# Whole-array state reads, batch 1 by half products, and a new order of all steps in an attention and PReLU-MLP kernel

## The chip, the cores and the metric

The kernel runs on one core of one Trainium2 chip. The metric is device time in microseconds (us) of one execution, the median over runs. The core has five engines with an instruction stream of their own each: TensorE (PE; its weight loads are listed as PEld), VectorE (DVE), ScalarE (ACT), GpSimd (POOL) and SyncE (SP, which here only issues DMAs). Each engine works through its stream in order and waits on semaphores for the others.

## The reference

Input x is (8 batches, 8 heads, 512 tokens, 64), state is (8, 8, 32, 64). Each batch and head computes attention both ways between its 512 tokens and its 32 states. The 544 rows of each batch, 512 wide, then go through an MLP with a leaky activation.

```python
scores = scale * np.matmul(x, state.transpose(0, 1, 3, 2))
a = softmax(scores)
xread = np.matmul(a, state)
scores2 = scale * np.matmul(state, x.transpose(0, 1, 3, 2))
a2 = softmax(scores2)
sread = np.matmul(a2, x)
x = concat([xread, sread], axis=2) as (4352, 512)
h = x @ w_in
g = np.maximum(h, 0.0) + alpha * np.minimum(h, 0.0)
return g @ w_out
```

(softmax over the last axis; d_ff is 2048; inputs and output are float32.)

## The kernel before

All matmuls take float16 and accumulate in float32. The work is cut into named steps, and one long string, `ORDER` (lines 17 to 96), lists them. Every token calls one function, which puts its instructions at the end of the streams of the engines it uses; there is no other scheduler. So the order of tokens is the order of work on each engine, DMA queues included. Numbers behind a step are batch, tile, part and PSUM bank (0 to 5; a further double bank is called "two"); a letter names the engine (a ACT, v DVE, p POOL).

**Loading.** Batch 0's x comes by two float32 loads from SP and is cast on chip (`cx`). The other batches (`lx`), the states (`lst`) and the MLP's weights in four parts each (`wi`, `wo`) come by POOL's queue, which casts on the way. In an x tile `xg` the token at j, p, r (two halves, 128 partitions, two neighbours) lies in partition p. `alpha` comes as a (128, 16) tile.

**Attention, tokens to states.** x is transposed, for batches 0 and 1 on PE (`xt`, copied by `xo`), for the others by a DMA (`xd`). `sc` are the scores, tiled onto parts of the PE array. `sb` (DVE block transpose), `smax`, `ssh` (shift, on POOL), `sexp` (ACT), `ssum`, `snorm` and `wb` (transpose back) make the weights `aT`. Batch 0 has another way, with scores per token (`tsc`) and PE transposes (`at`, `ao`). The token read is never formed: `m` multiplies the states of a batch by w_in (`mo` casts the result), and a first step takes aT times that.

**The MLP.** `F.b.jc` computes 128 columns of h for 512 tokens with two 512-column matmuls. `N` (ACT, relu of -h) and `G` (DVE) make g of it. `f`, `n`, `g` are the same by halves for batch 0's first columns. Batches 0 and 1 use `S.b.q.jc2`: two 512-column matmuls that accumulate an output tile, which `O` copies and stores. Batches 2 to 8 (8 stands for the state rows of all batches) use seven products of half matrices in place of eight (`P`, four 256-column matmuls each), with sums of w_out halves (`W`, on POOL, once) and of g halves (`U.b.i.c`, on POOL). `K` keeps a partial result in SBUF and `Q` adds it and stores a quarter.

**State reads.** `tm`, `nb`, `te`, `tsum`, `tn` make the softmax over tokens, `tt` transposes it by a DMA (SP) into `e2T`, and `rd` multiplies x by it. Each of its 32 matmuls has 64 columns of weights and 32 moving columns; the two heads of a pair lie side by side in the array (`tile_position=(0, D * i)`). `rdo` copies the result to `XS` on ACT, where the first steps of "batch 8" read it.

`Z.k.n` are n matmuls on a made-up pattern whose result nobody reads.

Of the kernel before, what the change touches and what calls it, by code (L numbers as in the profile page):

```python
# [21 lines left out]
xt.1.1.1.0 xt.1.0.0.3 wo.3 te.0.1 tsum.0 xo.1.0.0.v oma mo.0.0.a.0 m.1.0 f.0.1.0.4 sexp.0.1 ssum.0.1 xo.1.1.1.v  # L22
mo.1.0.a n.0.1.0 xt.1.0.1.1 xo.1.0.1.v f.0.0.0.2 n.0.0.0 xt.1.1.0.5 xo.1.1.0.v g.0.1.0.1 g.0.1.0.0 m.2.0.3.0 m.1.1
mo.1.1.a snorm.p.0.1 at.1.1 mo.2.0.a.0 ao.1.v g.0.0.0.1 m.0.1.5.4 mo.0.1.a.0 sc.1 tm.1 f.0.1.1.1 f.0.0.1.3 mo.0.1.a.1
F.0.4.5 F.0.5.4 mo.2.0.a.1 n.0.0.1 nb.1.a n.0.1.1 sb.1 te.1.0 g.0.0.0.0 g.0.1.1.0 te.1.1 S.0.2.1.0 g.0.1.1.1 F.0.6.2
N.0.6 g.0.0.1.1 g.0.0.1.0 tsum.1 G.0.6 N.0.5 G.0.5 S.0.2.0 S.0.1.1.1 m.0.2 mo.0.2.a F.0.7.3 N.0.7 smax.1 S.0.1.0 N.0.4
G.0.4 F.0.10.2 N.0.10 m.0.3 G.0.7 mo.0.3.a F.0.11.4 G.0.10 N.0.11 G.0.11 F.0.9.5 m.1.3 N.0.9 G.0.9 F.0.13.3 N.0.13
tn.0.1.p F.0.8.2 S.0.1.5 F.0.12.4 S.0.3.1.5 S.0.2.5 N.0.8 G.0.13 N.0.12 ssh.p.1 wo.1 sexp.1 F.0.15.3 S.0.3.5 G.0.8
S.0.2.4 mo.1.3.a G.0.12 ssum.1.2 F.0.14.4 S.0.2.6 S.0.1.6 m.1.2 S.0.3.6 S.0.3.4 snorm.v.1 lx.2 xd.2 wb.1 tn.1.1.a
S.0.1.4 W.1.1.p S.0.2.2 S.0.1.3 F.1.3.2 tn.0.0.a tt.0 mo.1.2.a N.0.14 S.0.2.3 G.0.14 N.0.15 G.0.15 F.1.10.4 F.1.2.3  # L30
tn.1.0.p N.1.3 G.1.3 N.1.2 G.1.2 S.0.2.7 O.0.2.a tt.1 S.0.3.0 N.1.10 F.1.4.2 N.1.4 G.1.10 G.1.4 S.0.1.7 F.1.9.0
F.1.11.3 N.1.9 G.1.9 F.1.1.4 N.1.1 G.1.1 S.0.1.2 N.1.11 W.3.0.p G.1.11 S.0.3.2 F.1.6.2 N.1.6 S.0.3.7 O.0.1.a sc.2 tm.2
m.2.2.0.4 rd.0.3 mo.2.2.a.1 sb.2 mo.2.2.a.0 rdo.0.a F.1.15.1 N.1.15 W.1.0.p G.1.15 nb.2.a S.0.0.5.4 F.1.8.0 N.1.8
# [66 lines left out]
def kernel(  # L100
# [118 lines left out]
    def fill(k, n):  # L219
        t = single(k, f"fill_{len(zs)}", [128, 256], F32)  # L220
# [565 lines left out]
```

## Time and profile before

| | us |
|---|---|
| runs (3) | 213.7, 214.05, 214.37 |
| median | 214.05 |
| profiled execution, first to last instruction (span) | 212.2 |

A time of its own is not listed for the profiled execution; the median stands 1.85 us above its span. Busy in that span: PE 203.6, DVE 174.8, POOL 165.0, ACT 150.3 us. The granted TensorE clock is 1.000.

In the views quoted below, a window row gives a stretch and its length, then the busy time of PE, PEld, DVE, ACT and POOL with their numbers of instructions, the clock, the busy share of the DMA engines and GB/s. A row of the chain gives start, duration, engine, tile and line. A timeline row gives start, duration, engine, line, operation, output and inputs, shape, count, and in brackets the idle time before and what ended it. A group row gives engine, operation, tiles, shape and count, then busy us and mean ns, then idle time before it and who ended that. In a row of waits stand total us, number and the longest.

### The profile page before, as it was taken

The page shows a single profiled execution, that of the slowest core. Times are in us where ns is not written, and L with a number is a line of the kernel's source. Part 1 is how long each engine was busy: PE and PEld are TensorE (multiplying, and loading weights), DVE is VectorE, ACT ScalarE, POOL GpSimd, SP SyncE. Part 2 cuts the span into 40 slices and gives each one's busy share as a digit, 9 for nine tenths or more (in the row PEclk, how much of TensorE's full clock was granted, in tenths as well). Part 3 has the DMA queues.
Part 4 walks back from the last instruction along what each step waited for, and adds up shares of the span by engine and source line. Part 5 has one row for each costly group of instructions (what it writes and reads, how often), then busy time and mean ns, then how long its engine had stood idle before and what let it go on. Part 6 is the DMA issues. An engine that isn't in the chain of part 4 may idle for free.

```text
span 212.2 us, 4985 instructions
## 1 busy us (share of the span) xinstructions
PE 203.6 (96%) x1974; PEld 132.5 (62%) x1974; DVE 174.8 (82%) x260; ACT 150.3 (71%) x292; POOL 165.0 (78%) x106
## 2 busy tenths in 40 slices
PE   7989899989999999999999999999999999999993
PEld 5655234444444545766668776767777678888882
DVE  0789999889999999999999999899997997423221
ACT  2489998789999869987998578878773866312110
POOL 8343074946749898969989999799979995999960
PEclk9999999999999999999999999999999999999999
DMA  6999979879599299634115581141305200121142
GB/s 172 208 183 205 207 114 163 127 186 114 172 111 258 29 150 149 151 78 123 53 49 57 95 249 48 21 131 21 82 8 145 102 0 0 53 99 49 43 158 99
DMA packets 52438, 23.68 MB, mean 112 GB/s; under 512 B 38464, under 2 KB 51392, under 8 KB 52416
## 3 DMA queue, kind: packets, MB, share of 16 engines
q0 software_dynamic: 18816, 8.09, 30.2%
q1 hardware_dynamic: 33328, 15.22, 28.5%
q8 instruction: 15, 0.25, 0.4%
q10 hardware_dynamic: 272, 0.07, 0.1%
q14 instruction: 7, 0.06, 0.1%
HBM read 17.31 MB, written 8.91 MB: 124 GB/s over the span
## 4 chain that ended last, share of the span: by engine, by line
PE 86%; DVE 6%; ACT 4%; DMA 2%; issue 1%; POOL 0%; POOLq 0%; ACTq 0%; DVEq 0%; SPq 0%
PE h L543 23%; PE px L701 21%; PE o L613 11%; PE pv L701 10%; PE py L701 5%; PE m_ps L494 4%; PE fill L223 4%; PE h L552 3%; PE sr_ps L467 2%; DMA e2T<-e 2%; DVE mx L368 1%; DVE g L599 1%; ACT m L520 1%; PE sc L303 1%; PE xT_ps L288 1%; ACT neg L596 1%
## 5 line engine op out<-in xcount | busy, mean ns | idle before, releaser
L599 DVE SCALAR_TENSOR_TENSOR g<-neg,oma_sb,h 128x512 f16<-128x512 f32 (+1 forms) x140 | 92.5, 710 | 9.5 <-ACT neg L596 8.3
L596 ACT ACTIVATE neg<-h 128x512 f32<-128x512 f32 (+1 forms) x140 | 75.3, 583 | 22.3 <-PE h L543 13.3
L543 PE MATMUL h<-aT,m 128*128 128x512 f16 x248 | 67.7, 379 | 1.3 <-DVE g L599 0.6
L701 PEld LDWEIGHTS <-gsum 128*128 128x128 f16 x416 | 40.3, 98 | 11.5 <-issue 1.3
L543 PEld LDWEIGHTS <-m 128*128 128x128 f16 x248 | 23.4, 98 | 20.1 <-issue 3.3
L701 PEld LDWEIGHTS <-g 128*128 128x128 f16 x312 | 30.3, 98 | 8.7 <-issue 0.8
L680 POOL TENSOR_TENSOR gsum<-g,g 128x1024 f16<-128x1024 f16 (+1 forms) x14 | 27.8, 1986 | 7.1 <-DVE g L599 4.8
L613 PE MATMUL o<-w_out_sb,g 128*128 128x512 f16 x128 | 33.1, 379 | 0.0
L680 POOL TENSOR_TENSOR gsum<-g,gsum 128x1024 f16<-128x1024 f16 (+1 forms) x14 | 27.8, 1991 | 1.9 <-PE px L701 1.6
L680 POOL TENSOR_TENSOR gsum<-g 128x1024 f16<-128x1024 f16 (+1 forms) x14 | 27.7, 1993 | 1.9 <-issue 1.9
L680 POOL TENSOR_TENSOR gsum<-gsum,g 128x1024 f16<-128x1024 f16 (+1 forms) x14 | 27.8, 1989 | 1.0
L701 PE MATMUL px<-ws,gsum 128*128 128x256 f16 x208 | 28.0, 273 | 0.0
L373 POOL TENSOR_TENSOR ts<-ts,mx 128x1024 f32<-128x1024 f32 x7 | 13.4, 1911 | 11.9 <-DVE mx L368 11.9
L613 PEld LDWEIGHTS <-g 128*128 128x128 f16 x128 | 12.2, 98 | 15.6 <-issue 1.2
L520 ACT CAST m<-m_ps 128x512 f16<-128x512 f32 x35 | 19.3, 598 | 3.7 <-PE m_ps L494 3.6
L717 ACT COPY kept<-px 128x512 f32<-128x512 f32 (+1 forms) x16 | 9.0, 566 | 14.1 <-PE px L701 11.0
L734 DVE TENSOR_TENSOR oq<-pv,kept 128x512 f32<-128x512 f32 (+1 forms) x14 | 9.1, 650 | 10.1 <-PE pv L701 7.2
L701 PE MATMUL pv<-ws,gsum 128*128 128x256 f16 x104 | 14.8, 273 | 0.0
L701 PE MATMUL px<-w_out_sb,g 128*128 128x256 f16 x104 | 14.6, 273 | 0.0
L701 PE MATMUL px<-w_out_sb,gsum 128*128 128x256 f16 x104 | 14.6, 273 | 0.0
L701 PE MATMUL py<-w_out_sb,g 128*128 128x256 f16 x104 | 14.5, 273 | 0.0
L701 PE MATMUL pv<-ws,g 128*128 128x256 f16 x104 | 14.3, 273 | 0.0
(74 smaller groups left out, 258.4 us busy)
## 6 DMA issues: line engine op xcount, KB each, us to landing
out_dram<-oq SPq DMA_DIRECT2D x24, 256.0 KB, 2.1
xg<-in_x_dram POOLq DMA_DIRECT2D x7, 512.0 KB, 6.1
w_in_sb<-in_moe_w_in_dram POOLq DMA_DIRECT2D x4, 512.0 KB, 14.3
w_out_sb<-in_moe_w_out_dram POOLq DMA_DIRECT2D x4, 512.0 KB, 14.0
out_dram<-osb SPq DMA_DIRECT2D x8, 256.0 KB, 3.1
x<-in_x_dram SPq DMA_DIRECT2D x2, 512.0 KB, 4.9
out_dram<-oq SPq DMA_DIRECT2D x4, 128.0 KB, 2.1
st<-in_state_dram POOLq DMA_DIRECT2D x1, 224.0 KB, 8.1
```

Source lines behind the costliest of these rows:

```text
L223: nc.tensor.matmul(t, pattern[:, :128], pattern, start=True, stop=True)
L373: engine(e).tensor_tensor(blocks(cols(live["ts", b], j, S)), blocks(scored(b, j)), over_blocks(cols(live["mx", b], j, S // N)), ALU.subtract,)
L494: nc.tensor.matmul(t[N * k : N * (k + 1), :], st_head(b, h)[64 * r : 64 * r + 64, :], w_in_sb[64 * r : 64 * r + 64, c, 512 * f : 512 * (f ...
L520: copier(e)(m_tile(b, f)[:, g, :], t[g])
L543: nc.tensor.matmul(h.rearrange("p (r j s) -> p r j s", r=2, j=2), ms[b, f][:, g, 128 * j : 128 * (j + 1)], weights(b, g), start=(g == 0), ...
L596: nc.scalar.activation(neg, h, RELU, bias=0.0, scale=-1.0)
L599: nc.vector.scalar_tensor_tensor(g_tile(b, jc), negs.pop((b, jc)), oma_sb[:, jc : jc + 1], hs.pop((b, jc)), ALU.mult, ALU.add,)
L613: nc.tensor.matmul(outs[b, q], g_tile(b, jc)[:, 128 * q : 128 * (q + 1)], w_out_sb[:, jc, :], start=not begun and jc == 2 * jc2, stop=left ...
L680: engine(e).tensor_tensor(t, x(), y(), op)
L701: nc.tensor.matmul(pbanks[b, name][:, i, :], of(b, c)[:, j, 128 * i : 128 * (i + 1)], moving[:, 4 * c + j, :], start=not begun and j == 0, ...
L717: copier(e)(t, pbanks[b, "x"])
L734: nc.vector.tensor_tensor(osb, pbanks[b, name], kept[b, add], ALU.add)
```

## The change

- **State reads.** Each matmul loads 128 neighbouring columns of x, its own 64 and the 64 beside them, and writes all 128 partitions. The head of a pair that wants the upper half starts 64 columns earlier. The result has a column block for each head of a pair, and only the half of the partitions that belongs to it is copied, so there are two copies per batch (16 in all, 14 on ACT and 2 on DVE).
- **Batch 1** uses the seven half products: 32 `S` and 4 `O` go, 28 `P`, 8 `U`, 3 `K` and 4 `Q` come.
- **Sums.** 15 of the 64 `U` are on DVE: one of batch 5, three of batch 6, four of batch 7 and seven of batch 8. The 8 `W` stay on POOL.
- **x in 1 KB runs.** The token at p, j, r is now row 4p + 2j + r, so a partition's four tokens lie together in memory; the output rows follow.
- **First x in four loads**: each half by two loads of four heads each, one on SP's queue and one on ACT's, the states between them on ACT's.
- **alpha** comes by four loads of 128-byte rows and is transposed on DVE.
- **Fills** have 512 columns; there are 6 at first and single ones later, where there were 16 of 256 and threes.
- **All places anew**: `ORDER` is another list of steps, with other banks and in part other engines.

The order before and after, up to batch 0's first read and the first w_out loads:

```diff
-wi.0 cx.0.1.a Z.0.3 cx.0.0.v Z.0.3 cx.1.0.v stc.a Z.0.3 stt.0 xt.0.0.1.1 Z.2.3 xt.0.0.0.2 cx.1.1.a xt.0.1.1.3 sbd.1.v
-lst lx.1 wi.1 wo.0 wi.2 xt.0.1.0.4 sbd.0.a xo.0.0.1.v tsc.0.1.5 xo.0.0.0.v tsc.0.0 wi.3 sto.v sc.0.0 xo.0.1.1.a
-xo.0.1.0.v sc.0.1 smax.0.0 ssh.v.0.0 sexp.0.0 tsc.1.0.1 Z.2.3 tm.0 Z.2.3 m.0.0.2.0 Z.3.3 mo.0.0.a.1 ssum.0.0 Z.3.3
-str.0.3 Z.4.3 tsc.1.1 str.1.4 nb.0.a te.0.0 sro.0.a smax.0.1 sro.1.v ssh.v.0.1 snorm.p.0.0 at.0.5 wo.2 ao.0.v
...
+Z.1.1 cx.0.0.v cx.0.1.v xt.0.0.0.2 xo.0.0.0.a xt.0.0.1.3 Z.4.1 stc.a Z.5.1 stt.0 cx.1.1.a sbd.1.a cx.1.0.v xt.0.1.0.1
+xo.0.1.0.a lst sbd.0.v xt.0.1.1.4 xo.0.0.1.v xo.0.1.1.a tsc.0.0.2 sto.a oma tsc.0.1 str.0.5 sro.0.a smax.0.0 ssh.v.0.0
+sexp.0.0 sc.0.1 sc.0.0 tm.0 wi.0 Z.3.1 lx.1 wi.1 wo.0 wi.2 ssum.0.0 snorm.p.0.0 str.1.1 tsc.1.0.4 sro.1.a tsc.1.1
+Z.0.1 smax.0.1 m.0.0.2.3 mo.0.0.v.1 Z.5.1 m.2.0.0.1 ssh.v.0.1 nb.0.a te.0.0 wi.3 te.0.1 tsum.0 tn.0.0.p mo.2.0.a.1
+at.0.5 tn.0.1.p ao.0.v sexp.0.1 m.1.0 mo.1.0.a mo.0.0.v.0 xt.1.0.1.3 xt.1.1.0.4 xo.1.0.1.v mo.2.0.a.0 ssum.0.1
+snorm.p.0.1 xt.1.0.0.1 xo.1.0.0.v f.0.1.0.5 f.0.0.0.2 xt.1.1.1.3 xo.1.1.1.v Z.0.1 n.0.0.0 g.0.0.0.0 m.1.1 m.0.1.1.0
+n.0.1.0 xo.1.1.0.v g.0.1.0.0 tt.0 mo.1.1.a at.1.3 ao.1.a sc.1 wo.1 g.0.1.0.1 Z.4.1 mo.0.1.a.0 W.1.0.p f.0.0.1.5
+f.0.1.1.3 mo.0.1.a.1 F.0.5.4 F.0.6.1 g.0.0.0.1 tm.1 sb.1 nb.1.v n.0.0.1 rd.0.2 g.0.0.1.0 n.0.1.1 N.0.5 G.0.5 S.0.2.1.0
+N.0.6 S.0.2.0 te.1.0 g.0.1.1.1 G.0.6 te.1.1 F.0.7.4 N.0.7 m.0.2 mo.0.2.a g.0.0.1.1 S.0.3.0.1 F.0.4.5 rdo.0.1.a lx.2
+wo.2 rdo.0.0.a g.0.1.1.0 N.0.4 S.0.3.1 smax.1 F.0.10.3 N.0.10 F.0.11.2 N.0.11 G.0.7 ssh.p.1 m.0.3 mo.0.3.a G.0.4
+tsum.1 G.0.10 F.0.9.4 N.0.9 G.0.11 F.0.8.5 G.0.9 N.0.8 G.0.8 S.0.2.2 tn.1.0.p S.0.3.3 F.0.12.3 N.0.12 G.0.12 F.0.15.2
...
```

The code:

```diff
-            x[b].rearrange("k (j p r) d -> p k j (r d)", j=2, r=2),
+            x[b].rearrange("k (p j r) d -> p k j (r d)", j=2, r=2),
...
-    def load_x0():
-        xgs[0] = att.tile([128, H, 2, 2, D], F16, name="xg_0", tag="xg", bufs=3)
-        for j in range(2):
-            t = att.tile([128, H, 2, D], F32, name=f"x0_{j}", tag="ts", bufs=2)
-            nc.sync.dma_start(
-                t, x[0, :, 256 * j : 256 * (j + 1), :].rearrange("k (p r) d -> p k r d", r=2)
-            )
+    def load_x0(j):
+        if j == 0:
+            xgs[0] = att.tile([128, H, 2, 2, D], F16, name="xg_0", tag="xg", bufs=3)
+        t = att.tile([128, H, 2, D], F32, name=f"x0_{j}", tag="ts", bufs=2)
+        x0s.append(t)
+        rows = x[0].rearrange("k (p j r) d -> j p k r d", j=2, r=2)[j]
+        for g in range(2):
+            queue = nc.sync if g == 0 else nc.scalar
+            queue.dma_start(t[:, 4 * g : 4 * g + 4], rows[:, 4 * g : 4 * g + 4])
...
-    alpha_sb = consts.tile([128, n_jc], F32)
-    nc.sync.dma_start(alpha_sb, moe_alpha.rearrange("(jc p) -> p jc", p=128))
-    pattern = consts.tile([128, 256], F16)
+    alpha_rows = consts.tile([128, 32], F32)
+    nc.vector.memset(alpha_rows, 0.0)
+    alpha_quarters = moe_alpha.rearrange("(jc q c) -> q jc c", q=4, c=32)
+    for q in range(4):
+        nc.sync.dma_start(alpha_rows[32 * q : 32 * q + n_jc, :], alpha_quarters[q])
+    pattern = consts.tile([128, 512], F16)
...
-    fill(0, 16)
+    fill(0, 6)
...
-        nc.vector.tensor_scalar(oma_sb, alpha_sb, -1.0, 1.0, ALU.mult, ALU.add)
+        alpha_cols = consts.tile([128, 32], F32)
+        nc.vector.transpose(alpha_cols, alpha_rows)
+        nc.vector.tensor_scalar(oma_sb, alpha_cols[:, :n_jc], -1.0, 1.0, ALU.mult, ALU.add)
...
-        t = live["sr", b] = single(bk, f"sr_ps{b}", [128, n_c, N], F32)
+        t = live["sr", b] = single(bk, f"sr_ps{b}", [128, n_c, 2, N], F32)
+        columns = xgs[b].rearrange("p k j r d -> p (k j r d)")
         for c in range(n_c):
             g = c // 2
-            for q in range(n_q):
-                r, j = divmod(q, 2)
-                for i in range(2):
-                    h = 2 * c + i
-                    k = (h - 4 * g) ^ g
+            for i in range(2):
+                h = 2 * c + i
+                k = (h - 4 * g) ^ g
+                for q in range(n_q):
+                    r, j = divmod(q, 2)
+                    at = D * (4 * h + 2 * j + r - i)
                     nc.tensor.matmul(
-                        t[D * i : D * (i + 1), c, :],
-                        xgs[b][:, h, j, r, :],
+                        t[:, c, i],
+                        columns[:, at : at + 2 * D],
                         e2T[:, g, q, N * k : N * (k + 1)],
                         start=(q == 0),
                         stop=(q == n_q - 1),
-                        tile_position=(0, D * i),
-                        skip_group_check=True,
                     )
...
-    def state_reads_out(b, e):
-        copier(e)(XS[:, :, b // 4, :, b % 4], live.pop(("sr", b)))
+    def state_reads_out(b, i, e):
+        rows = slice(D * i, D * (i + 1))
+        copier(e)(XS[rows, :, b // 4, :, b % 4], live["sr", b][rows, :, i])
```

More of the change, by code (lines that the diff above doesn't have):

```diff
@@ new lines @@
+N.7.2 G.7.2 U.6.1.1.p G.7.9 F.7.1.3 F.7.3.1 U.6.2.1.p P.6.6.1.1 P.6.6.0.1 N.7.1 F.7.6.5 N.7.3 G.7.3 G.7.1 N.8.0
+P.6.6.1.0 P.6.7.0.1.0 F.8.14.1 K.6.2.a G.8.0 N.7.6 N.8.14 F.7.12.3 N.7.12 G.7.12 F.7.13.2 P.6.5.0.1 N.7.13 P.6.7.1.1
+P.6.5.1.1 G.8.14 G.7.13 F.7.14.3 G.7.6 U.6.3.0.p N.7.14 G.7.14 F.7.11.1 P.6.5.1.0 F.8.6.2 N.7.11 F.8.10.5 G.7.11
+P.6.5.0.0 P.6.7.1.0 N.8.6 K.6.4.v P.6.7.0.0 Q.6.1.1 P.7.1.0.0.3 P.7.1.1.1 U.7.3.1.p F.8.1.1 P.6.4.0.1 U.7.1.0.v
+P.7.1.1.0 U.7.2.0.v P.6.4.1.0 G.8.6 N.8.10 P.6.4.0.0 G.8.10 P.6.4.1.1 P.7.2.1.1.2 Q.6.1.0 U.6.4.1.v P.7.2.0.0
@@ L624, in out_rows @@
         r, j = divmod(q, 2)
-        return out[b * S2 : b * S2 + S, :].rearrange("(j p r) d -> r j p d", j=2, r=2)[r, j]
+        return out[b * S2 : b * S2 + S, :].rearrange("(p j r) d -> r j p d", j=2, r=2)[r, j]
     def second_out(b, q, e):
@@ L721, in quarter_rows @@
         if b < B:
-            rows = out[b * S2 : b * S2 + S, :].rearrange("(j p r) d -> r p j d", j=2, r=2)
+            rows = out[b * S2 : b * S2 + S, :].rearrange("(p j r) d -> r p j d", j=2, r=2)
             return rows[th, :, :, cols]
```

146 lines of the change are left out of this document (68 added, 78 removed).

## The prediction

> **What bounds the kernel now.** I read the page's busy times and its chain first: which engine ends last.
>
> ```profile
> span 212.2 us, 4985 instructions
> PE 203.6 (96%) x1974; PEld 132.5 (62%) x1974; DVE 174.8 (82%) x260; ACT 150.3 (71%) x292; POOL 165.0 (78%) x106
> PE 86%; DVE 6%; ACT 4%; DMA 2%; issue 1%; POOL 0%; POOLq 0%; ACTq 0%; DVEq 0%; SPq 0%
> ```
>
> TensorE is 86% of the chain. A busy PE may still be slow, so the windows by stage come next (columns: stretch, its length, then PE, weight loads, DVE, ACT, POOL busy with counts, clock, DMA), and the pieces of the chain that show PE's pace.
>
> ```profile
> 20.00:30.00 10.00, 8.81 (x60) 3.17 (x59) 9.94 (x17) 9.95 (x21) 3.23 (x3) 1.00 1.06 176
> 30.00:40.00 10.00, 10.00 (x54) 4.36 (x53) 9.07 (x12) 8.28 (x14) 6.05 (x5) 1.00 0.97 129
> 40.00:60.00 20.00, 19.28 (x216) 8.68 (x215) 19.10 (x25) 17.95 (x36) 13.57 (x9) 1.00 0.81 149
> 60.00:80.00 20.00, 20.00 (x188) 9.55 (x187) 19.32 (x27) 16.98 (x35) 16.12 (x10) 1.00 0.99 145
> 80.00:95.00 15.00, 15.00 (x146) 9.73 (x145) 14.42 (x21) 13.76 (x27) 13.06 (x7) 1.00 0.75 124
> 140.00:180.00 40.00, 40.00 (x411) 29.16 (x409) 36.86 (x56) 27.82 (x58) 35.67 (x19) 1.00 0.21 61
> 180.00:205.00 25.00, 24.97 (x230) 22.24 (x228) 8.57 (x16) 5.71 (x14) 23.13 (x15) 1.00 0.20 72
> ```
>
> ```profile
> 39.71 4.34 DMA e2T<-e
> 44.10 0.68 PE sr_ps L467 x32
> 56.91 0.61 PE sr_ps L467 x32
> 60.56 1.73 PE o L613 x8
> 71.49 0.61 PE sr_ps L467 x32
> 72.44 0.61 PE sr_ps L467 x32
> 97.91 0.61 PE sr_ps L467 x32
> 150.78 1.12 PE sr_ps L467 x64
> 163.75 0.61 PE sr_ps L467 x32
> 184.93 1.75 PE px L701 x16
> 207.39 0.89 PE px L701 x8
> ```
>
> Three things are to be seen. From 30 us to 205 us PE is idle for 0.75 us in the stretches shown, 0.72 us of it in 40 to 60, where the chain goes through the transpose of batch 0's weights (e2T, 4.34 us). Inside that time PE is at its pace: 8 matmuls of 512 columns in 1.73 us are 0.216 us each, 16 of 256 columns in 1.75 us are 0.109 each. So what PE issues after 30 us is paid one for one. And in 20 to 30 us ACT (9.95) and DVE (9.94) are full while PE waits: there PE work is free, ACT and DVE work is not.
>
> **The change, part by part.** *Batch 1 by half products.* It drops 32 second steps of two 512-column matmuls, 64 x 0.216 = 13.8 us, and adds 28 product steps of four 256-column ones, 112 x 0.109 = 12.2 us: **-1.6 us** of PE in the full stretch.
>
> *State reads.* The eight reads take 0.68 + 5 x 0.61 + 1.12 = 4.85 us now, two 64-column halves of the array side by side. After, each is 32 matmuls one after another with a full 128x128 load and 32 moving columns; no row shows that form. The nearest have the same load and more columns:
>
> ```profile
> 9.35 0.29 PE L342 MATMUL tsc<-st_pairs,xT 128*128 128x64 f16 x4
> 14.71 0.62 PE L288 MATMUL xT_ps<-ident,xg 128*128 128x128 f16 x8 [0.67 <-DMA xg<-in_x_dram]
> L288 PE MATMUL xT_ps<-ident,xg x32: 216/219/230, 6.9 to 17.1; 128*128 128x128 f16 x32
> L342 PE MATMUL tsc<-st_pairs,xT x16: 193/193/203, 8.3 to 12.9; 128*128 128x64 f16 x16
> ```
>
> Taking one matmul's own time off each row, starts are (0.62 - 0.219) / 7 = 57 ns apart at 128 columns and (0.29 - 0.193) / 3 = 32 ns at 64. Halved again, 32 columns give 16 ns, the lower bound; if the load sets the pace it stays at 32, the upper. Both ends are one step of columns away, so I take the middle, 24 ns: 32 x 0.024 = 0.77 us a read, 6.15 us for eight, **+1.3 us** (ends 4.1 and 8.2 us: -0.75 and +3.35). The Trainium skill, "TensorE: Matmul & The Clock Gate", section "Wait — 56ns, not 53.3ns?", states that starts never come closer than about 25 ns however few columns there are; by it the reads are an estimated 6.4 us and the sum below is 0.25 us higher, while by the halving of the rows it is 2 us lower.
>
> *Read 0 goes early.* It stood behind the e2T transpose at 39.71, since ACT normalised half of batch 0's weights late. Now POOL normalises both right after the exponentials and the read stands behind the first F steps, ahead of the first second step. Its price, 0.77 us, falls into 20 to 30 us where PE has 10 - 8.81 = 1.19 us idle, and the 0.72 us of idle in 40 to 60 has no cause left: **-1.5 us** (ends: 0, if the transpose is late there too, and -1.9). SP issues that transpose behind nothing but the first loads, no longer behind batch 2's x transpose. Late next would be the reads of batches 1 and 2, whose transposes too are issued well before them.
>
> *Start.* The first x lands in halves on two queues, the weights' first load is issued behind the states, many casts change engine.
>
> ```profile
> 5.18 0.62 ACT L173 CAST xg<-x 128x512 f16<-128x512 f32 x1 [2.64 <-DMA x<-in_x_dram]
> 6.67 0.62 ACT L173 CAST xg<-x 128x512 f16<-128x512 f32 x1 [0.68 <-DMA x<-in_x_dram]
> 7.46 0.37 ACT L253 COPY st_pairs<-st_ps 64x256 f16<-64x256 f16 x1 [0.17 <-DVE st_pairs L253]
> 8.33 0.59 ACT L293 COPY xT<-xT_ps 128x512 f16<-128x512 f16 x1 [0.50 <-PE xT_ps L288]
> 10.48 0.63 ACT L382 ACTIVATE ts<-ts 128x512 f32<-128x512 f32 x1 [1.57 <-DVE ts L373]
> 12.63 1.06 ACT L270 COPY stT<-st_ps 128x896 f16<-128x896 f16 x1
> L520 DVE CAST m<-m_ps 128x512 f16<-128x512 f32 x3 | 2.1, 684 | 0.0
> L270 DVE COPY stT<-st_ps 128x896 f16<-128x896 f16 x1 | 1.1, 1134 | 0.0
> ```
>
> x's two halves arrive by 5.18 and 6.67 now; the bytes are the same, so I take the same. ACT then has, ahead of the first exponential, from about 6.1: an xT copy 0.59, the state cast (taken as 0.37, as the st_pairs copy), an x cast 0.62, st_pairs 0.37, two xT copies 1.18, the small stT copy (0.37 again) and the large one 1.06: 4.56 us, to 10.7, against 10.48 now: no gain. DVE gets two casts of m at 0.684 for a copy of 1.134: **+0.25 us** on the engine that is full there. Ends: -0.9 if two queues bring x sooner (half the 1.5 us between its landings and some), +1.5 (the spacing of x's landings again) if a load is late: POOL now issues the fourth w_in load behind the first norm, and the third and fourth w_out loads behind a w sum and batch 1's shift, where they went out ahead of these; what needs them, second steps and w sums, comes later in the new order too.
>
> *Work put on other engines.* Costed at nothing; the cover and its price:
>
> ```profile
> L680 POOL TENSOR_TENSOR gsum<-gsum,g 128x1024 f16<-128x1024 f16 x12 | 25.5, 2128 | 0.9
> L393 DVE TENSOR_TENSOR an<-ts,r 128x1024 f16<-128x1024 f32 x7 | 8.5, 1219 | 0.2
> L734 DVE TENSOR_TENSOR oq<-pv,kept 128x512 f32<-128x512 f32 x12 | 8.2, 688 | 7.3 <-PE pv L701 4.3 <-issue 2.8
> L478 ACT CAST XS<-sr_ps 128x128 f16<-128x128 f32 x8 | 3.6, 455 | 0.7 <-PE sr_ps L467 0.5
> POOL ts L373 <- DVE mx L368: 11.9, 3, 7.7
> xg<-in_x_dram POOLq DMA_DIRECT2D x7, 512.0 KB, 6.1
> ```
>
> POOL gets 8 sums more, 17.0 us, against 3.95 + 6.43 + 3.88 + 1.94 = 16.2 us idle between 30 and 95. At the end 15 sums leave it. DVE pays at most 1.22 us for a full one (the same tile, wider input), half for batch 8's: 12 of them come after about 180 us, 5 x 1.22 + 7 x 0.61 = 10.4 us, where DVE is idle for 25 - 8.57 = 16.4. Batch 1's three quarters on DVE are +2.1 us, three m casts and a kept copy moved to ACT -2.7. ACT's eight more state copies (0.455) and these casts lie in 140 - 180's 12 us of idle and the like before it. The 1 KB runs shorten x loads that land 6.1 us after issue, a batch or more ahead of use; their issue on POOL is at most as long. Alpha, out rows and the closing fills change nothing that ends last: the last px is followed by one copy and one store, as now.
>
> **Sum**: -1.6 + 1.3 - 1.5 + 0.25 = -1.55. The profiled span of 212.2 becomes 210.65; the median of the runs, 214.05, lies 1.85 above that span (what is around it), so 212.5.
>
> **Rivals.** *Reads stream at 16 ns.* For it: the pace halves with the columns in both rows. Reads fall by 2.05, read 0 hides 0.25 less, x perhaps 0.3 sooner: 210.4.
>
> *Reads keep 32 ns.* For it: two 64-column halves with 32 columns take 0.61 / 16 = 38 ns a pair now, so few columns don't buy pace there. +2.05 - 0.25: 214.3, no change.
>
> *POOL late with batch 1's sums (slower).* Product 3 of batch 1 needs the fourth sum, product 3 of batch 2 the same eight sums on; ahead stand the eight w sums. 17.0 us of sums meet 16.2 us of idle, of which the softmax shifts' waits for DVE's maxima, 11.9 - 7.7 = 4.2 us, may not go. Then POOL is up to 17.0 - 12.0 = 5 us late; PE has other products for some 2. PE stops for 3 us, in 65 to 95 us: 215.5. It decides from the point at which POOL loses 2 us of its idle time. Against: the order places those products last.
>
> *VectorE's sums block (slower).* Three of them (batch 5, two of batch 6) come in 140 to 180, where DVE has 3.1 us idle. Each costs 1.22 and, if it must wait for a POOL sum of 2.13 under way, about 1.1 more on average: 7.0 - 3.1 = 3.9 us by which G steps come late, of which products that need no new G cover one group or two (8 in 0.87 us, half of px's 1.75): 3 us on PE, 215.5. The Trainium skill, "SBUF — State Buffer", section "Who interferes with whom", states that a VectorE instruction with two SBUF inputs and a GpSimd one that reads SBUF exclude each other for the whole instruction. Nothing before shows it.
>
> **Chances.** Forecast (211.5 to 213.4) 0.44, reads at 16 ns 0.20, reads at 32 ns 0.14, POOL late 0.12, sums that block 0.10. About 0.3%, 0.64 us, is what a measurement can tell from no change. Faster: the first two and little else, 0.63; same: 0.15; slower: the last two, 0.22. The range, 210.0 to 215.3, takes in both ends of the reads with the start 0.4 better, and most of the POOL case.
>
> **What would show it.** Right: state reads of 0.6 to 0.9 us each, the first before 30 us; PE without a gap from about 30 us; the last product near 206.8. Wrong: reads of 1 us; PE waits on gsum between 65 and 95 us or on g after 140; VectorE sums that take over 2 us or start right when a POOL sum ends; the first h matmuls (15.87 us now) a microsecond later.
>
> ```profile
> 15.87 0.60 PE L565 MATMUL h<-aT,m 128*128 128x256 f16 x4 [0.20 <-DVE aT L357]
> ```

## The result, and the profile after

| | before | after |
|---|---|---|
| runs | 213.7, 214.05, 214.37, 214.97 | 237.81, 239.27, 241.8, 241.94 |
| median, us | 214.21 | 240.54 |
| profiled span, us | 212.2 | 237.5 |
| ratio, with its 95% interval | | 1.113 [1.107, 1.120] |

The kernel got slower by 11%, 24.2 us by the ratio (0.1131 x 214.21), where 212.5 us was forecast. The ratio leaves out the two runs above 241 us, so it says less than the medians' difference of 26.3. Below, what a kernel is over before is its ratio less one, times 214.2 us.

First the page of the kernel after: span, busy times, the chain by engine, and the granted clock in 40 slices of 5.9 us.

```profile
span 237.5 us, 5041 instructions
PE 208.1 (88%) x1992; PEld 137.7 (58%) x1992; DVE 188.6 (79%) x280; ACT 153.3 (65%) x299; POOL 157.1 (66%) x100
PEclk9979889758999999799999999999999999999998
PE 50%; DMA 19%; DVE 17%; ACT 4%; POOL 4%; issue 3%; DVEq 0%; POOLq 0%; ACTq 0%
```

TensorE's part of the chain fell from 86% to 50%, and DMA went from 2% to 19%. The pieces of that chain (start, length, what) say which DMAs:

```profile
16.55 11.28 DMA e2T<-e
27.88 1.02 PE sr_ps L478 x32
...
39.01 11.36 DMA xT<-xg
...
87.73 7.68 DMA e2T<-e
95.56 0.97 PE sr_ps L478 x32
106.53 6.93 DMA xT<-xg
```

They are the DMA transposes that SP issues: of the softmax weights (`tt`, into e2T) and of x (`xd`, into xT). The chain of before had one, 4.34 us long. Seen by tile, the transposes from issue to landing were, before:

```profile
L452 SPq DMA_TRANSPOSE e2T<-e x8: 1237/1265/1442, 39.7 to 157.8; - x8
DMA to landing us min/median/max: 3.0/3.3/4.5
```

and after:

```profile
L461 SPq DMA_TRANSPOSE e2T<-e x8: 1232/1314/2408, 16.6 to 183.2; - x8
DMA to landing us min/median/max: 3.1/3.8/11.3
```

The shortest are as short as they were; some take three times as long. For x, before:

```profile
L280 SPq DMA_TRANSPOSE xT<-xg x6: 1628/1733/1971, 37.9 to 121.6; - x6
DMA to landing us min/median/max: 3.6/3.8/5.3
```

and after:

```profile
L289 SPq DMA_TRANSPOSE xT<-xg x6: 1900/2237/4492, 39.0 to 141.7; - x6
DMA to landing us min/median/max: 4.2/4.5/11.4
```

TensorE works through its stream in order, so it stands at the first matmul that wants the late tile, and everything behind it stands too. The waits of TensorE in the kernel after (total, times, longest):

```profile
PE sr_ps L478 <- DMA e2T<-e: 10.2, 3, 5.0
PE sc L312 <- DMA xT<-xg: 6.2, 2, 4.4
```

TensorE is idle for 237.5 - 208.1 = 29.4 us, where it was 212.2 - 203.6 = 8.6; these two waits, 16.4 us, are most of the 20.8 between. By stage (columns as in the prediction's windows) the time goes where these stand, and late in the kernel a second time:

```profile
20.00:30.00 10.00, 4.59 (x65) 2.61 (x65) 7.29 (x13) 5.08 (x12) 5.13 (x4) 0.90 1.28 197
30.00:40.00 10.00, 9.70 (x60) 3.51 (x59) 6.15 (x10) 8.44 (x14) 4.59 (x5) 0.93 0.51 72
40.00:60.00 20.00, 13.76 (x106) 5.50 (x105) 11.22 (x14) 9.63 (x21) 10.20 (x7) 0.74 0.97 124
...
80.00:95.00 15.00, 12.19 (x142) 7.83 (x140) 13.92 (x19) 11.52 (x21) 14.60 (x10) 1.00 0.47 75
95.00:140.00 45.00, 41.83 (x409) 28.35 (x410) 36.86 (x51) 34.65 (x72) 34.50 (x21) 0.96 0.47 91
...
180.00:205.00 25.00, 23.43 (x223) 17.02 (x223) 22.86 (x34) 16.73 (x33) 11.90 (x6) 1.00 0.20 57
```

In 20 to 30 us TensorE works 4.59 us (before 8.81); in 40 to 60 it issues 106 matmuls where before it issued 216, and the clock there is 0.74. From 180 to 205 us VectorE is nearly full (22.86 of 25) and TensorE short of 1.6 us. Before, VectorE had 8.57 there, but the work that stands there now stood some 25 us earlier then: 155 to 180 us had 22.07.

**What the slow transposes share.** In the kernel before, loads on POOL's queue and transposes hardly met: the last w_out load had landed at 34.48 us and the x load issued at 29.45 at 37.79, the first transpose was issued at 37.87, and each later x load fell between transposes (two landed up to 0.9 us after one was issued). In the kernel after, five transposes are late. The first of them (16.55 us) runs among the weight loads, which last to 33.9 us; the second and third (37.59, 39.01) beside a w_out load issued at 36.01 and x loads issued at 39.61 and 45.47; the fourth (87.73) was issued within 0.1 us of an x load (87.66), the fifth (106.53) 1.4 us ahead of one (107.92). Counting the packets of the 16 DMA engines in the two traces, by the microsecond in which they start:

```
kernel, stretch        POOL's queue (loads)     SP's queue (transposes)
after   20 to 21 us    177 of 1024 B             67 of 256 B
after   21 to 22 us    152 of 1024 B            151 of 256 B
after   22 to 23 us    154 of 1024 B            156 of 256 B
after   23 to 24 us    147 of 1024 B            166 of 256 B
before  66 to 67 us    none                    1116 of 256 B
```

A transpose alone moves up to 1116 packets of 256 B in a microsecond. Here, beside a load, it gets one packet for one of the load's, and a load's packet is four times as large: 156 in a microsecond, a seventh. The Trainium skill, "DMA: Bandwidth & Descriptors", section "Queues, rings and completion order", states that each DMA engine goes round the queues that have work, a packet at a time; the near-equal counts from 21 to 24 us agree with it, if the trace's packets are that page's, which hold several descriptors each; no run shows whether they are.

Sharing by packets is not all of it. The same traces give, for each transpose, the time from its issue to its first packet, from there to the start of its last, and from there to its landing (us):

```
transpose, issued       to first packet   to last packet   to landing
before, e2T, 63.10      1.18              1.47             0.6
before, xT, 51.29       1.18              1.98             0.5
after, e2T, 16.55       3.92              6.68             0.7
after, e2T, 37.59       3.50              1.61             1.4
after, xT, 39.01        3.70              6.14             1.5
after, e2T, 87.73       1.19              2.69             3.8
after, xT, 106.53       1.48              2.62             2.8
```

Behind loads already under way the first packet itself comes 2.3 to 2.7 us later than alone, and the second transpose loses most of its time so; the last packet of the fourth starts after 3.9 us, and it is the landing that is held up. For the fifth the load is not shown to be the cause: in the kernel with the x loads apart its like (issued at 96.46) took 6.45 us with no packet of a load from issue to landing. What holds it up was not tried.

### The profile page after: what moved, and what is told of

The parts are those of the page before. It is cut to its first block, busy times and chain, and to the rows that moved or that the text cites. A ratio compares the mean times of both kernels' runs of the same rounds, so it can differ in the third digit from the quotient of the medians.

```text
span 237.5 us, 5041 instructions
## 1 busy us (share of the span) xinstructions
PE 208.1 (88%) x1992; PEld 137.7 (58%) x1992; DVE 188.6 (79%) x280; ACT 153.3 (65%) x299; POOL 157.1 (66%) x100
## 4 chain that ended last, share of the span: by engine, by line
PE 50%; DMA 19%; DVE 17%; ACT 4%; POOL 4%; issue 3%; DVEq 0%; POOLq 0%; ACTq 0%
PE h L553 14%; PE px L711 13%; DVE g L609 9%; DMA e2T<-e 8%; DMA xT<-xg 8%; PE pv L711 7%; PE o L623 5%; PE py L711 4%; PE h L562 3%; DVE gsum L690 2%; ACT neg L606 2%; PE sr_ps L478 2%; DMA x<-in_x_dram 2%; DMA alpha_rows<-in_moe_alpha_dram 2%; DVE oq L744 2%
## 5 line engine op out<-in xcount | busy, mean ns | idle before, releaser
L711 PEld LDWEIGHTS <-gsum 128*128 128x128 f16 x480 | 46.5, 98 | 14.8 <-issue 2.5
L711 PEld LDWEIGHTS <-g 128*128 128x128 f16 x360 | 35.0, 99 | 12.6 <-issue 3.1
L690 POOL TENSOR_TENSOR gsum<-g 128x1024 f16<-128x1024 f16 (+1 forms) x13 | 27.1, 2087 | 16.7 <-DVE g L609 14.4
L553 PEld LDWEIGHTS <-m 128*128 128x128 f16 x248 | 24.4, 100 | 20.0 <-issue 5.7
L711 PE MATMUL px<-ws,gsum 128*128 128x256 f16 x240 | 32.1, 273 | 0.0
L690 POOL TENSOR_TENSOR gsum<-g,g 128x1024 f16<-128x1024 f16 x13 | 27.6, 2127 | 4.4 <-DVE g L609 4.3
L690 POOL TENSOR_TENSOR gsum<-gsum,g 128x1024 f16<-128x1024 f16 x12 | 25.8, 2152 | 4.2 <-DVE gsum L690 3.4
L690 POOL TENSOR_TENSOR gsum<-g,gsum 128x1024 f16<-128x1024 f16 x11 | 23.3, 2126 | 4.0 <-PE px L711 3.9
L623 PE MATMUL o<-w_out_sb,g 128*128 128x512 f16 x64 | 19.4, 417 | 0.0
L711 PE MATMUL py<-w_out_sb,g 128*128 128x256 f16 x120 | 17.4, 277 | 0.5 <-DVE g L609 0.5
L478 PE MATMUL sr_ps<-e2T,xg 128*128 128x32 f16 x256 | 7.7, 178 | 10.3 <-DMA e2T<-e 10.2
L711 PE MATMUL px<-w_out_sb,g 128*128 128x256 f16 x120 | 16.7, 272 | 0.0
L711 PE MATMUL pv<-ws,g 128*128 128x256 f16 x120 | 16.7, 277 | 0.0
L422 DVE TENSOR_REDUCE nb<-sc 128x2 f32<-128x1024 f32 x8 | 9.7, 1211 | 8.4 <-PE sc L312 8.4
```

Source lines behind the costliest of these rows:

```text
L422: nc.vector.tensor_reduce(nb, live["sc", b].rearrange("p r j g s -> p g (r j) s"), AX.XY, ALU.max)
L478: nc.tensor.matmul(t[:, c, i], columns[:, at : at + 2 * D], e2T[:, g, q, N * k : N * (k + 1)], start=(q == 0), stop=(q == n_q - 1),)
L553: nc.tensor.matmul(h.rearrange("p (r j s) -> p r j s", r=2, j=2), ms[b, f][:, g, 128 * j : 128 * (j + 1)], weights(b, g), start=(g == 0), ...
L623: nc.tensor.matmul(outs[b, q], g_tile(b, jc)[:, 128 * q : 128 * (q + 1)], w_out_sb[:, jc, :], start=not begun and jc == 2 * jc2, stop=left ...
L690: engine(e).tensor_tensor(t, x(), y(), op)
L711: nc.tensor.matmul(pbanks[b, name][:, i, :], of(b, c)[:, j, 128 * i : 128 * (i + 1)], moving[:, 4 * c + j, :], start=not begun and j == 0, ...
```

## The experiments

Three theories were open after the traces. The first: the new order puts transposes beside loads, and what stands behind them is the loss. The second: it all follows from read 0 standing early, and the later waits are its echo. The third: the dearer reads, the clock, or the sums on VectorE and POOL make the time. Thirteen kernels ran:

| kernel | median us | ratio to before | over before, us |
|---|---|---|---|
| after | 240.54 | 1.113 [1.107, 1.120] | 24.2 |
| read 0 late | 238.12 | 1.108 [1.102, 1.114] | 23.1 |
| order of before, code of after | 217.88 | 1.018 [1.013, 1.022] | 3.8 |
| before with whole-array reads | 216.81 | 1.012 [1.009, 1.016] | 2.7 |
| all sums on POOL | 251.38 | 1.174 [1.169, 1.179] | 37.2 |
| all loads apart | 230.64 | 1.073 [1.067, 1.078] | 15.6 |
| x loads apart | 228.61 | 1.067 [1.063, 1.071] | 14.3 |
| fills ahead of the stands | 238.41 | 1.114 [1.111, 1.117] | 24.4 |
| before, extra loads (first try) | 214.85 | 1.002 [1.000, 1.004] | 0.4 |
| before, extra loads beside | 220.08 | 1.028 [1.022, 1.033] | 5.9 |
| transposes cleared | 226.18 | 1.056 [1.051, 1.062] | 12.1 |
| batch 1 by second steps | 230.09 | 1.075 [1.068, 1.082] | 16.1 |
| tiled reads | 222.67 | 1.038 [1.034, 1.043] | 8.2 |
| x transposes before stores | 223.32 | 1.041 [1.035, 1.047] | 8.7 |

### Is it read 0? Only read 0 moved back

```diff
-... sb.1 nb.1.v n.0.0.1 rd.0.2 g.0.0.1.0 ...        (rdo.0.1.a, rdo.0.0.a later)
+... F.0.12.3 N.0.12 G.0.12 rd.0.2 rdo.0.1.a rdo.0.0.a F.0.15.2 ...
```

> The changed kernel with read 0 and its two copies moved behind F.0.12, ahead of F.0.15. Theory 1 (TensorE, which works in order, stands at a read whose transposed weights have not landed, and all that is behind it comes late): the 5.0 us wait at 22.9 us goes, and with it the lateness of batch 1's weights and of batch 2's transposed x behind it, and the half clock after 45 us: 8 to 14 us less, 226 to 232. Theory 2 (each transpose beside a load is slow by itself, whatever stands ahead): only the first wait goes, 4 to 5 us, about 235. Theory 3 (the reads, the products or VectorE's sums cost it): within 2 us of 240.

The intervals of the two kernels overlap: 1 us of 24, if any. By its time alone, 238.12 us, it falls to Theory 3 of the expectation and not to Theory 2; the waits tell more. The stand at read 0 went, and TensorE reached the next late tile sooner; in its chain an x transpose now took 16.16 us, and the waits changed places:

```profile
PE sc L311 <- DMA xT<-xg: 10.8, 2, 6.8
PE sr_ps L477 <- DMA e2T<-e: 5.9, 2, 3.6
```

16.7 us in all, for 16.4 before it. The later waits are no echo of the first, and the theory of an echo falls.

### Is it the order or the code? The order of before with the code of after

```diff
 ORDER = """
-(the order of after)
+(the order of before, its banks, engines and fills; rdo.b.0.a rdo.b.1.a for each rdo.b.a; batch 1 by S)
```

> The order, banks, engines and fills of before (batch 1 by second steps, all sums on POOL) with the new reads, x in 1 KB runs, x in four loads and the new alpha. If the order is what costs (theories 1 and 2), this is near before: reads at 25 ns a matmul add 1.5 us, the rest is hidden, 214.5 to 216.5. If the new code itself costs, it is over 220.

The code (reads, x in 1 KB runs, first x in four loads, alpha's way) costs 3.8 us in the old order; 217.88 lies outside both ranges that were expected. So the new order, batch 1's half products and the sums on VectorE with it, carries about 20 of the 24. In the kernel with the order of before, with x in 1 KB runs, no transpose took over 6.2 us (x transposes 4.5 at the median, before 3.8), the clock was 1.0 throughout, and DMA is 6% of the chain. So the longer runs of x alone are not what makes transposes of 7 to 11 us.

### What do the reads cost? Before, with the whole-array reads alone

```diff
-    nc.tensor.matmul(t[D * i : D * (i + 1), c, :], xgs[b][:, h, j, r, :], ..., tile_position=(0, D * i))
+    nc.tensor.matmul(t[:, c, i], columns[:, at : at + 2 * D], ...)
```

> Before with nothing but the whole-array reads and their two copies. A read was 0.61 us and shows 0.80 (32 at 25 ns) after: 8 x 0.19 = 1.5 us less a little where the array need not change its tiling, so 215 to 216. If whole-array matmuls save more between neighbours than they cost, 213 to 214.

+2.7 us [2.0, 3.3], about 1 more than expected. Its timeline has the new price of a read

```profile
57.92 0.97 PE L469 MATMUL sr_ps<-e2T,xg 128*128 128x32 f16 x32
73.11 0.96 PE L469 MATMUL sr_ps<-e2T,xg 128*128 128x32 f16 x32
```

and that of before the old one:

```profile
56.84 0.68 PE L467 MATMUL sr_ps<-e2T,xg 128*64 128x32 f16 x32
```

0.29 us a read, 2.3 for eight. One matmul takes 0.176, so starts are (0.97 - 0.176) / 31 = 25.6 ns apart. The Trainium skill's 25 ns ("TensorE: Matmul & The Clock Gate", section "Wait — 56ns, not 53.3ns?") agrees. The old reads' matmuls, in pairs side by side, started closer than that, 16.0 ns apart on average (see why the prediction was wrong). What is left to +2.7 is within its interval.

### Are VectorE's sums too dear? All sums on POOL

```diff
-U.5.3.1.v ... U.8.4.0.v      (15 tokens)
+U.5.3.1.p ... U.8.4.0.p
```

> The changed kernel with all 64 sums of g halves on POOL. Theories 1 and 2: nothing up to 140 us changes; VectorE's sums of 1.5 to 2 us show in the chain only after 175 us, so 3 us less to 1 us more, POOL being full again at the end: 237 to 241. If sums on VectorE cost much through a wait for POOL: 5 us or more less.

Outside both expectations, 13 us slower than after: in this order POOL can't take them (16% of the chain is POOL then, and TensorE waits 9.0 us for POOL's sums). So it does not give a price for the sums on VectorE, some of which are slower than was costed (last section); the waits on e2T and xT are as long as in the kernel after, 9.7 and 7.3 us, so the sums did not make those.

### Is it the loads? Loads and transposes moved apart

Two kernels. In the first, the x loads alone:

```diff
-... O.0.3.a lx.4 F.1.10.2 ... S.0.1.2 lx.3 G.1.10 ...
+... O.0.3.a F.1.10.2 ... S.0.1.2 lx.3 lx.4 G.1.10 ...
-... tn.3.0.p lx.5 F.2.15.1 ...            ... xd.5 lx.6 U.2.4.1.p ...
+... rdo.2.1.a ... rdo.2.0.a lx.5 ...      ... rdo.3.0.a lx.6 ...
```

> The kernel after, with only the x loads of batches 4, 5 and 6 moved as in the run with all loads apart; weights, read 0 and everything else as after. Theory: the first transpose still takes 10 to 12 us and read 0 still stands (about 6 us lost by 30 us), the second still meets the last w_out quarter, the others take 3.3 to 5 us; time 226 to 234 us, between the kernel after and the run with all loads apart, and the difference to the latter is what the start costs. Rival (the start alone decides, the later waits are its echo): within 2 us of the kernel after.

9.9 us less than after, by the places of three tokens that no engine computes anything for. TensorE's waits on e2T and xT fell from 16.4 to 4.4 + 3.5 = 7.9 us. Its row for 40 to 60 us, 13.76 and 0.74 in the kernel after:

```profile
40.00:60.00 20.00, 16.28 (x115) 7.11 (x116) 13.81 (x20) 12.75 (x28) 12.82 (x9) 0.83 0.88 159
```

The fourth late transpose fell from 7.7 to 3.1 us. That is the largest single piece found. Not all went as expected: the first took 7.8 us, not 10 to 12 (the last piece of x landed at 9.40 in this execution, so it was issued 2.3 us later, with more of the loads done), and the fifth, with no load beside it now, still 6.45. In the second, also the weights and read 0:

```diff
-... te.0.0 wi.3 te.0.1 ...   ... sc.1 wo.1 ...   ... lx.2 wo.2 ...   ... wo.3 N.0.15 ...
+... te.0.0 wi.3 wo.1 wo.2 wo.3 te.0.1 ...        ... lx.2 ...
```

> The kernel after, with only the places of loads and of read 0 changed: the three last w_out quarters are issued right behind the last w_in quarter, x of batch 4 behind x of batch 3, x of batch 5 behind read 2, x of batch 6 behind read 3, and read 0 stands behind S.0.3.3 as in the run with read 0 late. Theory (a transpose that runs beside a load lands late, and PE stands in order behind it): of the transposes after the first none lands more than 5 us after its issue (after: 6.6, 11.4, 7.7, 6.9), TensorE waits under 5 us in all on e2T and xT after 25 us (after: about 15), the granted clock does not go to half after 40 us, time 217 to 225 us. Rival (the order is too tight for VectorE and POOL whatever the transposes do): transposes get short, but the waits turn up at g and gsum, time over 231 us.

A miss: 1.3 us more than the x loads alone, not less, with intervals that overlap. The chain shows why:

```profile
19.84 12.11 DMA e2T<-e
...
37.23 10.19 DMA xT<-xg
...
98.27 6.42 DMA xT<-xg
```

The weights ahead of x of batch 2 made that x land at 37.07 us; its transpose was issued at 37.23, beside the loads of batches 3 and 4 (35.59 and 40.40). One collision had been traded for another. The transpose at 98.27 is the fifth one again: no load's packet runs beside it.

### Is it the clock? Fills ahead of the four stands

```diff
+Z.2.24 before rd.0.2; Z.2.24 before sc.2; Z.0.20 before rd.3.0; Z.4.16 before sc.5
```

> The kernel after, with fill matmuls (128x512, results unused) put ahead of read 0 (24), score step 2 (24), read 3 (20) and score step 5 (16), where TensorE stood. Theory: the loss is the waiting, and half clock after it a smaller part: transposes stay at 7 to 11 us, the granted clock stays at 1.0 except for under 6 us in all (after: about 20 us at half), time 231 to 237 us. Rival (the half clock behind each stand is most of the loss): 222 to 228 us. If the fills cost more than they save, over 240 us.

The fills keep the clock up, in 40 to 60 us at 0.91 for 0.74:

```profile
40.00:60.00 20.00, 18.37 (x134) 7.92 (x132) 11.50 (x16) 9.97 (x22) 10.49 (x7) 0.91 1.00 127
```

and the time stays: one interval lies inside the other, and the 231 to 237 us expected were missed. The longest transposes still take 12.3 (e2T) and 11.2 us (xT). So fills get nothing back here; whether the half clock cost nothing or the fills ate what they saved can't be told from this.

### Can it be made to happen in the kernel before?

```diff
+    def extra_load(i):
+        nc.gpsimd.dma_start(st..., x[i, :7, :256, :]...)          # 224 KB into a tile nobody reads any more
```

> The kernel before, with two extra loads on POOL's queue (224 KB of x in 512 B runs of the source, into the tile of the states, which nobody reads any more): one right behind the token norm of batch 2, at its transpose, and one right ahead of the transpose of batch 4; their data is not used. Theory (a load beside a transpose stretches it): the transposes of batches 2 and 4 take 5 to 8 us in place of 3.3, the neighbours without a load stay at 3 to 5; the order of before issues each well ahead of its reader, so the time grows by at most 2 us, 213.5 to 216.5 us. Rival (transposes are slow in the new order for another reason): they stay within 3.0 to 4.6 us.

Inconclusive: POOL reached the tokens earlier than thought, and the first load had 2 us beside a transpose, the second 0.8, before the transpose's first packet. The first transpose took 4.0 us for 3.3, the second 3.3 as before. Two loads each (224 and 112 KB; the data isn't used), placed by what POOL was doing when the transposes go out:

```diff
-... tn.3.1.p ...        ... U.2.4.1.p ...
+... tn.3.1.p ex.0 ...   ... U.2.4.1.p ex.1 ...
```

> The kernel before with two pairs of extra loads (224 KB and 112 KB of x, data not used), this time issued by POOL behind the token norms of batch 3, so beside the x transpose of batch 4 and the transpose of batch 3, and behind the sum U.2.4.1, so beside the transpose of batch 4 and the x transpose of batch 6. In the first try (214.85 us) the loads had ended before: only 2 us of one ran beside a transpose, which took 4.0 us for 3.3. Theory: those four transposes take 5 to 8 us (before: 3.8, 4.6, 3.2, 3.8), all others as before; time 213.5 to 217 us. Rival: they stay within 0.7 us of their times of before.

The x transposes, by tile (landing, and TensorE's wait on xT):

```profile
L288 SPq DMA_TRANSPOSE xT<-xg x6: 1934/2094/4072, 38.0 to 127.1; - x6
  DMA xT<-xg: 3.2, 2
DMA to landing us min/median/max: 4.3/5.5/9.8
```

That of batch 4, issued at 65.41, took 9.8 us (before 3.8), that of batch 3's weights, behind it on SP's queue, 6.1 (before 4.6), that of batch 4's weights 5.9 (before 3.2), the x transpose of batch 6 6.0 (before 3.8). Not all others stayed as before: the other four x transposes, two of them ahead of the first extra load, took 0.65 to 1.15 us longer than before, for which I have no cause; those of batches 4 and 6 grew by 6.1 and 2.3. The kernel before became 5.9 us slower, twice the most that was expected: the margin in its order is smaller than I thought. TensorE's waits on xT and e2T make 3.2 + 0.9 = 4.1 us of it (before 0.7); 1.2 us (before none) are waits on POOL's sums; issuing the four loads took POOL 4 us. The window in which the first pair ran:

```profile
70.00:80.00 10.00, 7.03 (x112) 3.69 (x111) 7.25 (x9) 5.04 (x9) 9.90 (x6) 1.00 1.30 146
```

against that of before:

```profile
70.00:80.00 10.00, 10.00 (x129) 5.14 (x128) 9.70 (x13) 7.27 (x15) 8.70 (x5) 1.00 0.67 93
```

3.0 us of TensorE, 2.25 behind the late xT and 0.7 behind the late e2T. In 71 to 72 us 417 packets of POOL's queue (128 B) started and 435 of SP's (256 B), near one for one again; from 68 to 70 us the shares change (427 to 209, then 248 to 453). This shows, without the new order, that loads beside transposes make them late and stop TensorE.

### What is left?

The collisions that the last two kernels kept were cleared one by one:

```diff
-... wi.3 wo.1 wo.2 wo.3 ...         ... xd.6 P.2.7.1.0 Q.2.1.1 ...
+... wi.3 lx.2 wo.1 wo.2 wo.3 ...    ... P.2.7.1.0 Q.2.1.1 xd.6 ...
 (lx.3 behind W.2.0.p, lx.4 behind W.3.1.p, xd.3 and xd.4 behind lx.4)
```

> The run with all loads apart (230.6 us), with x of batch 2 loaded ahead of the last three w_out quarters, x of batches 3 and 4 one weight sum later each, and the x transpose of batch 6 one output later than that of batch 5. There the x transpose of batch 2 still took 10.2 us beside those two loads and that of batch 5 took 6.4. Theory: the x transpose of batch 2 takes under 6 us, that of batch 5 under 5, TensorE's wait on xT falls from 8.3 us to under 4, time 223 to 227 us. Rival (these waits are only moved to VectorE, which is as late): transposes short, time 228 us or more.

12.1 us less than after, so half the loss is gone by places of loads, transposes and one read, and the wait on xT fell to 2.7 us. In the stages:

```profile
30.00:40.00 10.00, 9.02 (x89) 4.06 (x88) 7.90 (x13) 8.64 (x14) 10.00 (x7) 1.00 1.19 180
40.00:60.00 20.00, 20.00 (x174) 9.51 (x171) 19.41 (x27) 17.84 (x36) 15.86 (x10) 1.00 0.91 159
...
95.00:140.00 45.00, 41.49 (x428) 28.70 (x426) 39.56 (x52) 34.71 (x69) 37.79 (x22) 1.00 0.44 95
140.00:180.00 40.00, 38.16 (x356) 27.64 (x355) 38.50 (x54) 26.77 (x52) 31.90 (x17) 1.00 0.24 61
```

Before, 95 to 140 us was full:

```profile
95.00:140.00 45.00, 44.93 (x423) 31.44 (x422) 43.50 (x60) 36.81 (x71) 41.68 (x22) 1.00 0.39 89
```

With the transposes cleared, 40 to 60 us is full again; 95 to 180 is not (79.65 of 85 us, before 84.93). The x transpose of batch 2 took 6.4 us (expected: under 6), that of batch 5 still 6.25 (expected: under 5), with no load beside it. Two attempts on the rest:

```diff
 (transposes cleared, and)
-    nc.tensor.matmul(t[:, c, i], columns[:, at : at + 2 * D], ...)
+    nc.tensor.matmul(t[D * i : D * (i + 1), c, :], xgs[b][:, h, j, r, :], ..., tile_position=(0, D * i))
```

> The run with the transposes cleared (226.2 us), with the state reads as 64x64 tiles again and one copy for each batch. Theory (the whole-array reads cost what they cost in the order of before, 2.3 us): 223 to 225 us. Rival (in the new order they lie in TensorE's idle time): 225.5 to 227 us.

The reads are in the 128x64 tiles of before here. -3.9 us, so the whole-array reads, with their second copies, cost about what they cost in the old order (+2.7) or somewhat more. And:

```diff
-... Q.2.0.0 ... xd.5 U.2.4.1.p ...    ... Q.2.1.1 xd.6 ...
+... xd.5 Q.2.0.0 ...                  ... xd.6 P.2.7.1.0 Q.2.1.1 ...
```

> The run with the transposes cleared (226.2 us), with the x transposes of batches 5 and 6 issued one output store earlier, since there that of batch 5 took 6.25 us behind a 256 KB store on the same queue and TensorE lost 5 us from 90 to 110 us. Theory: both take under 5 us, 222.5 to 225 us. Rival (VectorE and the scores set that stretch anyway): 225.5 us or more.

A time as the theory had it (8.7 us over before, with an interval clear of that of the kernel it came from), but not by its mechanism: in the profiled execution (226.16 us, the median being 223.32) neither transpose took under 5 us; they took 8.05 and 6.32. On SP three stores of batch 1 stood ahead of the first instead of one of batch 2, and POOL had issued an x load at 87.83, which landed at 94.50:

```profile
82.89 6.53 SPq L744 DMA_DIRECT2D out_dram<-oq  x3
89.52 5.50 SPq L288 DMA_TRANSPOSE xT<-xg  x1
95.11 0.55 SPq L744 DMA_DIRECT2D out_dram<-oq  x1
95.77 3.18 SPq L288 DMA_TRANSPOSE xT<-xg  x1
```

They were issued earlier in the work, though, and that was enough in this execution: TensorE's wait on xT, 2.7 us in the kernel it came from, is gone, and 95 to 180 us is nearly full, 83.45 of 85 us for 79.65:

```profile
95.00:140.00 45.00, 44.21 (x473) 30.97 (x472) 42.36 (x58) 37.66 (x73) 40.76 (x23) 1.00 0.51 110
140.00:180.00 40.00, 39.24 (x365) 28.37 (x363) 38.50 (x53) 27.16 (x54) 31.91 (x17) 1.00 0.24 61
```

So an earlier issue, not a shorter transfer, is what fits; no second trace confirms it. Last, whether batch 1's eight sums made POOL late (an edit of the kernel with the x loads apart):

```diff
-P.1.1.0.0.5 ... U.1.1.1.p ... K.1.1.a ... Q.1.0.0      (28 P, 8 U, 3 K, 4 Q of batch 1)
+S.1.1.6.5 ... O.1.0.v                                 (32 S, 4 O in their places)
```

> The run with the x loads apart (228.6 us), with batch 1's token rows by 32 second steps of two 512-column matmuls in the places of its 28 half products, so without its eight sums on POOL (17 us of POOL). Theory that POOL's extra sums do no harm: the matmuls cost 1.6 us more, 229 to 231.5 us. Rival (batch 1's sums make POOL and then VectorE late, which is the loss after 95 us): 222 to 226 us.

1.8 us more, as the theory had it, with intervals that overlap. POOL's busy time fell from 157.2 to 140.3 us and nothing got faster: its sums were covered.

## Why the prediction was wrong, step by step

- **The step that failed is the term at nothing, "Work put on other engines"**, and with it that the sum has no term at all for the new places of loads and transposes. The x loads were passed over because they land "a batch or more ahead of use". That looked at who reads the load; the harm is to what moves beside it. The order carries about 20 of the 24 us, and the places of three x loads alone were worth 9.9. In "Start" I named the weight loads that go out late and asked again only for their users.
- **"Read 0 goes early", -1.5 us, rests on the same omission**, in two sentences: "the 0.72 us of idle in 40 to 60 has no cause left", and "the reads of batches 1 and 2, whose transposes too are issued well before them". I asked when a transpose is issued and behind what on SP's queue, and took its 3 to 5 us from the trace of before as its price. That price held while no load was under way. Its end "0, if the transpose is late there too" counted lateness as a lost gain of 1.5, where TensorE's waits came to 10.2 us on e2T and 6.2 on xT. Moving read 0 back was worth 1 us, if any, so this term by itself is not the loss.
- **State reads +1.3**: mechanism right, size wrong. 0.97 us a read where 0.77 was taken: +2.3 by the rows, +2.7 by the run. The 24 ns taken for the distance of starts was near the 25.6 measured; more of the error lies in the base. The old read takes 0.68 us in the timeline, not the 0.61 of the chain, and its starts are (0.68 - 0.183) / 31 = 16.0 ns apart on average, where I set 0.61 / 32 = 19 against them. The difference is 9.6 ns a matmul, not 5.
- **Batch 1 by half products -1.6**: supported by the run that undid it (+1.8, interval too wide for more). *POOL late with batch 1's sums* falls with the same run.
- **Start +0.25**: too small, inside its ends. The last piece of the first x, the second load on ACT's queue, landed at 7.15 us in the kernel after and at 9.03 in the order of before with the new code, where x was complete at 6.65; "I take the same" was wrong. The first h matmuls came at 16.78 and 17.62 for 15.87. In the old order the code beside the reads costs 3.8 - 2.7 = 1.1 us, with intervals that overlap.
- *VectorE's sums block*: the blocking is real (last section), but the waits on e2T and xT stay without those sums. What the sums cost in the new order stays open; from 180 to 205 us, where VectorE is nearly full, TensorE loses 1.6 us. *Reads at 16 ns* and *at 32 ns* both fall by the 25.6.
- None of the rivals had the mechanism that the runs showed: one engine's DMA queue made slow by another's. Of the signs of being wrong, the reads of 1 us, the later h matmuls and a VectorE sum over 2 us were seen, all three on small terms; none of the signs was a late DMA.

**What stays open.** With transposes clear and tiled reads the kernel is still 8.2 us over before, half products included. Its trace shows some pieces. TensorE waits 2.4 us, up to 20.82, for batch 0's normalised weights from POOL, which issues four loads from 15.22 to 18.35 ahead of them. From 95 to 180 us it is idle for 5.3 us, 3.3 of them from 95 to 110, behind x transposes and a copy of ACT. The kernel with the x transposes before stores, on whole-array reads, is idle there for 1.6 us only; the two edits were not put together. About 1 us may be the code at the start. The rest lies in the order. No version tried beats the kernel before.

## What to carry to other kernels

A DMA's time in a trace holds for the company it had there. When an order of work is changed, list for each transfer that someone will stand behind what else is in flight at that moment on any queue, not only what is ahead of it on its own; here a transfer in 256 B packets fell to a seventh of its pace beside one in 1024 B packets. And before trusting a margin, put a load beside it once: two late tiles cost TensorE 3 us here.

## What the runs showed of the hardware that was not expected

- **One packet for one, and a late first packet.** 156 packets of 256 B against 154 of 1024 B in a microsecond, 435 of 256 B against 417 of 128 B; and the first packet up to 3.9 us behind the issue, where it is 1.2 alone. A 512 KB transpose beside a load took 6 to 16 us for 3.6 to 5.3.
- **Sums on VectorE beside sums on POOL.** The timeline of VectorE in the kernel after, near its end:

```profile
189.82 1.72 DVE L690 TENSOR_TENSOR gsum<-gsum,g 128x1024 f16<-128x1024 f16 x1
192.12 1.95 DVE L690 TENSOR_TENSOR gsum<-g,gsum 128x1024 f16<-128x1024 f16 x1
207.07 2.15 DVE L690 TENSOR_TENSOR gsum<-g,g 128x1024 f16<-128x1024 f16 x1
209.25 0.69 DVE L690 TENSOR_TENSOR gsum<-gsum,g 128x1024 f16<-128x1024 f16 x1
```

and of POOL:

```profile
188.87 2.13 POOL L690 TENSOR_TENSOR gsum<-g,g 128x1024 f16<-128x1024 f16 x1 [0.43 <-DVE g L609]
191.07 2.45 POOL L690 TENSOR_TENSOR gsum<-gsum,g 128x1024 f16<-128x1024 f16 x1
...
206.54 2.12 POOL L690 TENSOR_TENSOR gsum<-g,g 128x1024 f16<-128x1024 f16 x1
```

The same sum takes 0.69 us on VectorE alone, and 1.72 to 2.15 when a POOL sum is under way; it then ends about 0.55 us after POOL's has ended (207.07 + 2.15 = 209.22, POOL's at 208.66). I had costed it at 1.22, with 1.1 for the wait. The Trainium skill's rule that the two exclude each other ("SBUF — State Buffer", section "Who interferes with whom") is borne out here; it was a side matter in this kernel.
